# Queries on 128 partitions and token blocks by parity, in a fused attention and gated feed-forward kernel

## Chip, cores and metric

The kernel runs on one core of one Trainium2 chip. The metric is the device time of one execution in microseconds (us). It was 236.85 us before the change, the median of three runs (236.81 to 237.19). A profile of one execution gives the time of every instruction and of every DMA packet.

## What is computed

Eight batches, eight heads, 576 tokens, head size 64, 32 memory slots. Keys and values are first condensed to 32 memories per head by a softmax over `phi`; the queries attend to the memories; the heads are put side by side to 512 columns, and a gated feed-forward block of width 1536 follows.

```python
a    = softmax(phi, axis=2)                    # [b, h, s, 32]
k_m  = einsum('bhsm,bhsd->bhmd', a, k)         # [b, h, 32, 64]
v_m  = einsum('bhsm,bhsd->bhmd', a, v)
attn = softmax(q @ k_m^T / sqrt(64))           # [b, h, s, 32]
x    = (attn @ v_m) as [b * s, h * 64]         # [4608, 512]
out  = (silu(x @ w_gate) * (x @ w_val)) @ w_out
```

Inputs and output are float32 in memory; the loads of q, k, v and the weights cast to bfloat16 on the way.

## The kernel before

**Staging.** The program is written out by hand in its order (`manual_schedule`); each engine runs its own instructions in that order and waits on semaphores. The batches are pipelined. The prologue (lines 870 to 975) loads and prepares batches 0 and 1, with filler matmuls (`warm`) between; then both go through the first feed-forward half together. The main loop runs over b = 2 to 7. In each turn it makes the scores of batch b, in between runs matmuls of the last feed-forward product of batch b - 1, and then the 24 gate/value slots of batch b, into which the k/v sums and other preparations of batch b + 1 are spread.

**Queries.** A batch's q is loaded to `t_q` with a head's tokens on 96 partitions, six consecutive rows each (`P, J = 96, 6`). For batches 0 to 2 `load_q_group` loads it in two DMAs, even and odd heads, and later batches have one (`load_q`); all are on POOL's queue, in program order with phi, k, v and the weights. The scores need q with the head size on the partitions. For batches 0 to 2 TensorE transposes it (`q_T`, L381): four steps of six transposes of 96 x 128, each step for two pairs of heads into one PSUM bank, and a copy to `t_qT` by VectorE or ScalarE (L394, L392). From batch 3 on, one DMA transpose on SP's queue does it (`load_qT`, L121). A pair of rows (r = 0, 1) fills 128 partitions, so the columns of `t_qT` are tokens by row pair.

**Attention.** `scores(b, g)` (L404) makes eight matmuls for the even or the odd heads; ScalarE takes the exp (`t_E`, L415). The sum over the memories is inverted either by TensorE and ScalarE (`z_inv`, batches 0 and 1, `t_lz`) or by VectorE (`z_inv_v`), and `norm` multiplies (`t_A`, L455). `r` splits the tokens into two halves of 288.

**Feed-forward.** The condensed values are multiplied into the weights first (`u_round`, `u_item`, `u_three`: `p_u`, L475, emptied to `t_U` by L495 to L501). A slot (`gv_slot`, L518) makes a gate product, its silu on ScalarE (`t_sg`, L535), a value product, and VectorE's multiplication to `t_h` (L541). The last product goes by a scheme with seven instead of eight block products (`products`, L739): it needs sums and differences of blocks of `t_h` (`t_S`, L563, L605) and of `w_out` (`t_T`). A batch's 576 tokens make two blocks of 256; the remaining 64 of four batches together make a "quad" (`xs`, L595, `quad_sums`), done in batch 4's and in the last slots and at the end. Units of these products are taken from a list, `backlog`, and spread between the other work as filler. For batch 2 the list is set from the last product of batch 1:

```python
        if b == 2:
            norm(2, 1)
            u_three(2)
            backlog = one[36:]
```

**PSUM.** There are eight banks, handed out in the order in which they were given back (`bank`, `done`). Evacuated results go to `t_o` tiles with three buffers.

**Stores.** `store` (L699) splits 128 tokens at the borders of 96, so that a block of 128 leaves in two DMAs (96 and 32, 64 and 64, or 32 and 96 rows). They go out on SP's queue; in the last quad some of the stores of 64 tokens are on ScalarE's queue. In the last batch and the last quad, halves of 256 columns are stored on their own.

Of the kernel before, what the change touches and what calls it, by code (L numbers as in the profile page):

```python
# [14 lines left out]
def kernel(  # L15
# [23 lines left out]
    B, H, S, D = q.shape  # L39
    M = phi.shape[3]  # L40
    DM, DF = moe_w_gate.shape
    P, J = 96, 6
    JK = 9
    NG = 2
    NP = H // 2
# [15 lines left out]

    ctx.enter_context(tc.manual_schedule())

    out_r = out.rearrange("(b p j) c -> b j p c", b=B, p=P, j=J)


    phis, kvs, qs, qTs = {}, {}, {}, {}
# [33 lines left out]
    def load_v(b):  # L101
        nc.gpsimd.dma_start(out=kvs[b][:, 1], in_=head_pairs(v[b]))  # L102

    def load_q_group(b, g):

        if g == 0:
            qs[b] = inp.tile([P, NG, NP, J * D], BF16, tag=f"q{Q_SLOT[b]}", bufs=1, name="t_q")
        nc.gpsimd.dma_start(  # L108
            out=qs[b][:, g],
            in_=q[b].rearrange("(i g) (p j) d -> g p i (j d)", g=NG, p=P)[g],  # L110
        )

    def load_q(b):
        t = inp.tile([P, H, J * D], BF16, tag=f"q{Q_SLOT[b]}", bufs=1, name="t_q")
        nc.gpsimd.dma_start(out=t, in_=q[b].rearrange("h (p j) d -> p h (j d)", p=P))
        qs[b] = t

    def load_qT(b):

        t = att.tile([128, H, 3, P], BF16, tag="qT", name="t_qT")  # L120
        nc.sync.dma_start_transpose(  # L121
            out=t.rearrange("p h j t -> p (h j) t"),
            in_=qs[b].rearrange("p h f -> p (h f)"),
        )
        for i in range(NP):
            qTs[b, i] = t[:, 2 * i:2 * i + 2].rearrange("p h j t -> p h (j t)")

    W = {}

# [242 lines left out]
        done(p)  # L372
        scaled.add(b)

    def q_T(b, g, n, eng="v"):


        pq = bank([128, 2, HALF], BF16, "p_q")
        for i in range(2):
            for jj in range(3):  # L380
                nc.tensor.transpose(  # L381
                    pq[:, i, P * jj:P * (jj + 1)],
                    qs[b][:, g, 2 * n + i, 2 * D * jj:2 * D * (jj + 1)],
                    ident[0:P, 0:P],
                )
        if g == 0 and n == 0:
            box["qT"] = att.tile([128, H, 3, P], BF16, tag="qT", name="t_qT")
            for i in range(NP):
                qTs[b, i] = box["qT"][:, 2 * i:2 * i + 2].rearrange("p h j t -> p h (j t)")
        t = box["qT"].rearrange("p (i g) j t -> p g i (j t)", g=NG)[:, g, 2 * n:2 * n + 2]  # L390
        if eng == "a":
            nc.scalar.copy(out=t, in_=pq)  # L392
        else:
            nc.vector.tensor_copy(out=t, in_=pq)  # L394
        done(pq)

    def gv_banks():
# [2 lines left out]
    def scores(b, g):  # L400
        p = gv_banks()
        for i in range(NP):
            for r in range(2):
                nc.tensor.matmul(  # L404
                    p[r][32 * i:32 * i + 32, 0:HALF],
                    lhsT=kTs[b][64 * r:64 * r + 64, g, 32 * i:32 * i + 32],
                    rhs=qTs[b, i][64 * r:64 * r + 64, g],
                    start=True,
                    stop=True,
                    tile_position=(64 * r, 32 * i),  # L410
                )
        e = att.tile([128, 2, HALF], BF16, tag=f"E{g}", name="t_E")
        for r in range(2):
            scale = rks[b][:, g:g + 1] if b in rks else sm_scale
            nc.scalar.activation(out=e[:, r], in_=p[r][:, 0:HALF], func=AF.Exp, scale=scale)  # L415
        done(*p)
        es[b, g] = e
# [166 lines left out]
    def blocks(b, c):  # L584

        x = hts[b, c].rearrange("p (m e) t -> p e m t", e=2)
        return [x[:, e, :, 256 * n:256 * n + 256] for n in range(2) for e in range(2)]

    def chunk_done(b, c):

        if b % 2 == 0 and c == 0:
            xs[b // 2] = hpool.tile([128, NJF, 2, 64], BF16, tag="xs", name="t_x")

        def ends():
            nc.gpsimd.tensor_copy(  # L595
                out=xs[b // 2][:, 4 * c:4 * c + 4, b % 2], in_=hts[b, c][:, :, S - 64:S]
            )
# [12 lines left out]

        end = c + 1 == NCH
        fourth = b in (3, 7)
        if (b, c) in ((0, 2), (1, 1), (1, 2)):
            late.append(lambda *part: sums(nc.gpsimd if b else nc.vector, *part))
        elif b < 2:
            sums(nc.gpsimd)
        elif end:
            sums(nc.vector)
            if b + 1 == B:
                second.pop()(nc.vector, (2, 3))  # L620
                wait_for(Ss[b, 1][0:1, 3, 0, 0:1])
            else:
                wait_for(t[0:1, 3, 0, 0:1])
                second.pop()(nc.gpsimd, (3, 2))
        else:
            if c:
                sums(nc.gpsimd, (0, 1))
                second.append(sums)
            else:
                sums(nc.gpsimd)  # L630
        if end and b > 1 and not fourth:
            late.append(ends)
        else:
# [15 lines left out]
    def quad_sums(qd):  # L649
# [22 lines left out]
                    subtract(nc.gpsimd, t[:, 2], A12, t[:, 1])  # L672

    beside_sums = {
        (0, 0): lambda: (load_phi(3, nc.gpsimd), load_q_group(2, 0)),
        (1, 0): lambda: (load_q_group(2, 1), load_q(3)),
        (0, 1): lambda: (load_k(3), load_v(3)),
    }

    turn = [1]  # L680

    def token_segments(b, t0, count):
        segs = []
        t = t0
        while t < t0 + count:
            blk, pp = divmod(t, P)
            n = min(P - pp, t0 + count - t)
            segs.append((t - t0, n, b, 2 * (blk % 3) + blk // 3, pp))
            t += n
        return segs  # L690

    def store(t_o, b, t0, count, row=0, cols=slice(0, 512), queues=None):

        for r0, m, bb, jj, pp in token_segments(b, t0, count):
            eng = nc.sync
            if queues:
                turn[0] += 1
                eng = queues[turn[0] % len(queues)]
            eng.dma_start(out=out_r[bb, jj, pp:pp + m, cols], in_=t_o[row + r0:row + r0 + m])  # L699

    def products(b, by_hand, quad=None):

# [6 lines left out]
        def A(e, n):  # L709
            if quad is not None:  # L710
                return lambda c, m, u: xs[2 * quad + n][:, 4 * c + 2 * m + e].rearrange(
                    "p a t -> p (a t)"
                )
            return lambda c, m, u: hts[b, c][
                :, 2 * m + e, 256 * n + 128 * u:256 * n + 128 * u + 128
            ]

        def Sx(n):
# [52 lines left out]
                done(mine[home])  # L771

        def both(name, t0, cols):
            for u in range(U):
                store(mine[name][:, u, cols], b, t0 + 128 * u, 128, cols=cols)

        def c11():
            t = tile_of("o1", (128, 2, DM), tag="to")
# [17 lines left out]
            both("o2", 256, slice(0, DM))  # L796

        def leftover(name, room, half, cols):
            queues = dict(c22=(nc.scalar,), c21=(nc.scalar, nc.sync)).get(name) if end else None

            def run():
                if room:
# [12 lines left out]
                    done(home)  # L815
                for k in range(2):
                    x = 4 * quad + 2 * (name > "c20") + k
                    store(t, x, S - 64, 64, 64 * k, cols, queues)

            return run  # L820

# [18 lines left out]
        return first + five + six + three + seven + four, ops  # L840

    def q_items(b, evac):
        return [
            lambda g=g, n=n: q_T(b, g, n, evac[2 * g + n]) for g in range(NG) for n in range(2)
        ]

    def u_item(b, c, evac="avav"):

# [51 lines left out]
    load_phi(1, nc.scalar)  # L900
    exp_tables()
    load_k(0)
    for g in range(NG):
        load_q_group(0, g)
    load_k(1)
    nc.vector.memset(bones, 0.0)
    nc.vector.memset(ones1, 1.0)
# [6 lines left out]
    for b in range(2):  # L914
        phi_zeros(b, nc.vector)
        phi_exp_masked(b)
    for g in range(NG):
        load_q_group(1, g)
    load_v(0)
    load_v(1)  # L920
    for half in range(2):
# [14 lines left out]

    warm(104)
    k0, k1 = k_items(0, "vvvv"), k_items(1, "vvvv")
    q0, q1 = q_items(0, "vvvv"), q_items(1, "vvvv")
    run(k0)  # L940
    warm(8)
    run(k1[:1])
    warm(4)
    run(q0[:2])
    warm(2)
    scores(0, 0)
    run(q0[2:])
    warm(2)
    z_inv(0, 0)
    scores(0, 1)  # L950
# [1 line left out]
    run(k1[1:])  # L952
    warm(3)
    z_inv(0, 1)
    run(q1[:2])
    warm(2)
    scores(1, 0)
    norm(0, 0)
    run(q1[2:])
    norm(0, 1)  # L960
    warm(3)
    z_inv(1, 0)
# [175 lines left out]
```

## Time and profile before

| | |
|---|---|
| median of three runs | 236.85 us (236.81 to 237.19) |
| profiled execution, its own time | 236.93 us |
| its span in the profile | 235.1 us |
| TensorE matmuls | 225.3 us, 96% of the span, 2842 instructions |
| VectorE / ScalarE / POOL | 185.2 / 173.0 / 143.9 us (79 / 74 / 61%) |
| granted TensorE clock | 0.999 |
| DMA | 36.84 MB, 157 GB/s on average |
| loads of q | 5 DMAs of 576 KB, 6 of 288 KB |
| stores on SP's queue | 23 of 192 KB, 40 of 64 KB, 14 of 128 KB, two each of 96 and 32 KB |

Busy times overlap, since the engines work at the same time. The matmuls are pipelined and the end of each is modelled, so that 96% does not mean that TensorE is at its peak. What counts is the chain of work that ended last. The time outside the span, 1.8 us, lies before and after the profiled instructions.

### The profile page before, as it was taken

To read this page: it belongs to the slowest core of one execution; us is meant where nothing else is said; L and a number is where in the kernel's file an instruction comes from. 1 tells how busy PE (TensorE), PEld (TensorE's weight loads), DVE (VectorE), ACT (ScalarE), POOL (GpSimd) and SP (SyncE) were. 2 spreads that over 40 slices of the span, in tenths; PEclk is the share of its full clock that TensorE was granted. 3 is DMA by queue.
4 is the path that set the end of the run, shared out by engine and by line. 5 is a ranking of instruction groups with operands and counts; after the bars stand their busy time and mean duration, and the time that the engine had idled before them with its cause. 6 is when DMAs were issued, how large, how long until landed. Compare 5 with 4: busy or idle time off the path is not lost.

```text
span 235.1 us, 7317 instructions
## 1 busy us (share of the span) xinstructions
PE 225.3 (96%) x2842; PEld 170.5 (73%) x2842; DVE 185.2 (79%) x425; ACT 173.0 (74%) x368; POOL 143.9 (61%) x193
## 2 busy tenths in 40 slices
PE   7998899999999999999999999999999999999992
PEld 2555467778886677887788787887788778878881
DVE  4157699999976797999798667998799879977732
ACT  2758889987447888978896668978898789677220
POOL 8542526999099069664976689464845494039390
PEclk9999999999999999999999999999999999999999
DMA  6999999999996992999199945999022803212125
GB/s 208 205 205 207 198 208 207 225 239 249 206 195 168 251 222 22 268 219 189 31 191 249 237 132 85 246 230 121 6 86 74 142 0 93 60 46 76 42 62 167
DMA packets 42594, 36.84 MB, mean 157 GB/s; under 512 B 15424, under 2 KB 37952, under 8 KB 42560
## 3 DMA queue, kind: packets, MB, share of 16 engines
q0 software_dynamic: 21440, 22.42, 54.4%
q1 hardware_dynamic: 20352, 13.18, 25.0%
q10 hardware_dynamic: 768, 0.79, 1.0%
q8 instruction: 22, 0.36, 0.6%
q14 instruction: 12, 0.10, 0.1%
HBM read 42.47 MB, written 9.44 MB: 221 GB/s over the span
## 4 chain that ended last, share of the span: by engine, by line
PE 86%; DMA 8%; POOL 2%; DVE 1%; issue 1%; POOLq 0%
PE p_g L518 21%; PE p_v L518 21%; PE p_os L739 20%; PE p_oc L739 10%; DMA t_kv<-in_v_dram 8%; PE p_u L475 5%; PE p_oa L739 5%; PE p_kv L234 2%; POOL t_q L108 1%; PE p_g L404 1%; POOL t_kv L98 1%; PE p_q L381 0%; DVE t_bkv L270 0%; POOL t_kv L102 0%; PE p_mT L323 0%
## 5 line engine op out<-in xcount | busy, mean ns | idle before, releaser
L541 DVE TENSOR_TENSOR t_h<-t_sg,p_v 128x288 bf16<-128x288 bf16 x192 | 82.2, 452 | 17.6 <-PE p_v L518 7.2
L518 PEld LDWEIGHTS <-t_U 128*128 128x128 bf16 x768 | 73.7, 98 | 23.9 <-issue 3.3
L535 ACT ACTIVATE t_sg<-p_g 128x288 bf16<-128x288 f32 x192 | 74.3, 423 | 18.4 <-PE p_g L518 12.0
L518 PE MATMUL p_g<-t_A,t_U 128*128 128x288 bf16 x384 | 77.4, 286 | 1.1 <-DVE t_U L499 0.7
L518 PE MATMUL p_v<-t_A,t_U 128*128 128x288 bf16 x384 | 77.2, 286 | 0.0
L739 PEld LDWEIGHTS <-t_S 128*128 128x128 bf16 x384 | 37.4, 98 | 4.5 <-issue 0.2
L605 POOL TENSOR_TENSOR t_S<-t_h 128x512 bf16<-128x512 bf16 x17 | 19.6, 1154 | 31.4 <-DVE t_h L541 31.4
L739 PEld LDWEIGHTS <-t_h 128*128 128x128 bf16 x288 | 26.9, 98 | 8.9 <-issue 5.3
L495 ACT CAST t_U<-p_u 128x512 bf16<-128x512 f32 x53 | 28.0, 607 | 6.9 <-PE p_u L475 6.9
L739 PE MATMUL p_os<-t_T,t_S 128*128 128x256 bf16 x192 | 23.7, 273 | 0.0
L563 POOL TENSOR_TENSOR t_S<-t_S,t_h 128x512 bf16<-128x512 bf16 x17 | 19.6, 1154 | 1.3
L563 POOL TENSOR_TENSOR t_S<-t_h 128x512 bf16<-128x512 bf16 x16 | 18.4, 1150 | 0.0
L563 POOL TENSOR_TENSOR t_S<-t_h,t_S 128x512 bf16<-128x512 bf16 x16 | 18.4, 1150 | 0.0
L475 PE MATMUL p_u<-W,t_kT 64*32 64x512 bf16 (+1 forms) x416 | 15.9, 363 | 0.1
L739 PE MATMUL p_os<-t_T,t_h 128*128 128x256 bf16 x96 | 15.3, 274 | 0.0
L889 PE MATMUL p_warm<-bones 128*128 128x512 bf16 (+2 forms) x43 | 12.8, 427 | 1.7 <-DVE bones L912 1.7
L499 DVE CAST t_U<-p_u 128x512 bf16<-128x512 f32 x19 | 12.4, 684 | 2.0 <-PE p_u L475 2.0
L739 PE MATMUL p_oc<-t_T,t_S 128*128 128x256 bf16 x96 | 12.0, 273 | 0.0
L739 PE MATMUL p_oa<-WO,t_h 128*128 128x256 bf16 x96 | 11.8, 273 | 0.0
L739 PE MATMUL p_oc<-WO,t_S 128*128 128x256 bf16 x96 | 11.8, 272 | 0.0
L739 PE MATMUL p_os<-WO,t_h 128*128 128x256 bf16 x96 | 11.8, 272 | 0.0
L455 DVE TENSOR_TENSOR t_A<-t_E,t_lz 128x576 bf16<-128x576 bf16 x16 | 11.4, 740 | 0.3 <-ACT t_lz L431 0.3
(107 smaller groups left out, 315.1 us busy)
## 6 DMA issues: line engine op xcount, KB each, us to landing
t_kv<-in_k_dram POOLq DMA_DIRECT2D x8, 576.0 KB, 11.0
t_kv<-in_v_dram POOLq DMA_DIRECT2D x8, 576.0 KB, 14.9
out_dram<-t_o SPq DMA_DIRECT2D x23, 192.0 KB, 2.6
t_phi<-in_phi_dram POOLq DMA_DIRECT2D x6, 576.0 KB, 9.9
t_q<-in_q_dram POOLq DMA_DIRECT2D x5, 576.0 KB, 8.5
out_dram<-t_o SPq DMA_DIRECT2D x31, 64.0 KB, 2.3
out_dram<-t_o SPq DMA_DIRECT2D x14, 128.0 KB, 3.7
t_q<-in_q_dram POOLq DMA_DIRECT2D x6, 288.0 KB, 11.4
```

The source lines that it names most:

```text
L234: nc.tensor.matmul(p[g][32 * i:32 * i + 32, 0:n], lhsT=phi_of(b, g, j, i), rhs=kvs[b][64 * g:64 * g + 64, w0:w1, i, j * D:(j + 1) * D], st ...
L455: nc.vector.tensor_tensor(out=a, in0=es.pop((b, g)), in1=lzs.pop((b, g)), op=ALU.mult)
L475: nc.tensor.matmul(p[g][32 * i:32 * i + 32, o:o + n], lhsT=kTs[b][64 * g:64 * g + 64, 2, 32 * i:32 * i + 32], rhs=w_part(w, c, i, g, halve ...
L495: nc.scalar.copy(out=t, in_=p)
L499: nc.vector.tensor_copy(out=t, in_=p)
L518: nc.tensor.matmul(p[:, 0:HALF], lhsT=Us[b, c, g][:, o // 2, which, 128 * (o % 2):128 * (o % 2 + 1)], rhs=atts[b, g][:, r], start=(g == 0) ...
L535: nc.scalar.activation(out=sg, in_=gate[:, 0:HALF], func=AF.Silu)
L541: nc.vector.tensor_tensor(out=dst, in0=sg, in1=val[:, 0:HALF], op=ALU.mult)
L563: eng.tensor_tensor(out=out, in0=x, in1=y, op=ALU.subtract)
L605: eng.tensor_tensor(out=t[:, 0], in0=A21, in1=A22, op=ALU.add)
L739: nc.tensor.matmul(mine[home][:, u], lhsT=lhs(c, m, u), rhs=rhs(c, m), start=fresh and u == 0, stop=(k == 5), skip_group_check=u == 1 or n ...
L889: nc.tensor.matmul(p[:, 0:128 * a], lhsT=bones, rhs=x.to_broadcast([128, a, 128]) if a > 1 else bones, start=True, stop=True,)
```

## The change

A partition of `t_q` now holds 36 consecutive rows of a head: partition 16 h + c has the rows 36 c to 36 c + 35 of head h, so that a batch's q is one contiguous [128, 2304] array and comes in one DMA. Two consecutive rows (r = 0, 1) are 128 columns; 18 such column blocks (s) are transposed as 128 x 128 squares, in three steps of six for batches 0 to 2 and by one DMA transpose for the others. The scores of a head read 16 columns from each of the 18 blocks (`q_of`). Token 36 c + 2 s + r now stands at r * 288 + 16 s + c. The two blocks of 256 tokens are thus those with even and with odd rows (r), s below 16; the remainder is s = 16 and 17 of both. A block of 128 tokens (eight s, sixteen c) is stored by one DMA, and so are the remainder's 64 tokens of one batch; in the last quad the first batch's go on SP's and the second's on ScalarE's queue. Last, the six remaining units of batch 1's last product are run before batch 2's slots instead of being spread into them.

```diff
-    out_r = out.rearrange("(b p j) c -> b j p c", b=B, p=P, j=J)
+    out_r = out.rearrange("(b c s r) k -> b r s c k", b=B, c=NC, s=NS)      # NS, NC = 18, 16
...
+    def load_q(b):
+        t = inp.tile([128, NS * 128], BF16, tag=f"q{Q_SLOT[b]}", bufs=1, name="t_q")
         nc.gpsimd.dma_start(
+            out=t,
+            in_=q[b].rearrange("h s d -> (h s d)").rearrange("(p f) -> p f", p=128),
         )
...
     def load_qT(b):
+        qTs[b] = att.tile([128, NS, 128], BF16, tag="qT", name="t_qT")
+        nc.sync.dma_start_transpose(out=qTs[b], in_=qs[b])
+
+    def q_of(b, i, g, r):
+        h = NG * i + g
+        return qTs[b][64 * r:64 * r + 64, :, NC * h:NC * h + NC]
...
+    def q_T(b, n, eng="v"):
+        k = NS // 3
+        pq = bank([128, k, 128], BF16, "p_q")
+        for x in range(k):
+            y = k * n + x
+            nc.tensor.transpose(pq[:, x], qs[b][:, 128 * y:128 * y + 128], ident)
+        if n == 0:
+            qTs[b] = att.tile([128, NS, 128], BF16, tag="qT", name="t_qT")
+        copy(eng, qTs[b][:, k * n:k * n + k], pq)
         done(pq)
...
-                    rhs=qTs[b, i][64 * r:64 * r + 64, g],
+                    rhs=q_of(b, i, g, r),
...
-        return [x[:, e, :, 256 * n:256 * n + 256] for n in range(2) for e in range(2)]
+        return [x[:, e, :, HALF * n:HALF * n + 256] for n in range(2) for e in range(2)]
...
-                out=xs[b // 2][:, 4 * c:4 * c + 4, b % 2], in_=hts[b, c][:, :, S - 64:S]
+                out=xs[b // 2][:, 4 * c:4 * c + 4, b % 2].rearrange(
+                    "p o (s r t) -> p o s r t", s=2, r=2
+                ),
+                in_=hts[b, c].rearrange("p o (r s t) -> p o s r t", r=2, s=NS)[:, :, 16:],
...
+    def store_block(t_o, b, n, cols):
+        for u in range(2):
+            nc.sync.dma_start(out=out_r[b, n, 8 * u:8 * u + 8, :, cols], in_=t_o[:, u, cols])
+
+    def store_leftover(t_o, b, cols, eng):
+        rows = out_r[b, :, 16:NS, :, cols].rearrange("r s c k -> s r c k")
+        eng.dma_start(out=rows.rearrange("s r c k -> (s r) c k"), in_=t_o)
...
-            queues = dict(c22=(nc.scalar,), c21=(nc.scalar, nc.sync)).get(name) if end else None
+            engs = (nc.sync, nc.scalar) if end else (nc.sync, nc.sync)
...
-    q0, q1 = q_items(0, "vvvv"), q_items(1, "vvvv")
+    q0, q1 = q_items(0, "vvv"), q_items(1, "vvv")
...
-    run(q0[:2])
+    run(q0)
     warm(2)
     scores(0, 0)
-    run(q0[2:])
...
-    run(q1[:2])
+    run(q1)
     warm(2)
     scores(1, 0)
     norm(0, 0)
-    run(q1[2:])
...
-            kv, q2 = kv_items(2), q_items(2, "aava")
+            kv, q2 = kv_items(2), q_items(2, "aaa")
...
-            backlog = one[36:]
+            run(one[36:])
```

More of the change, by code (lines that the diff above doesn't have):

```diff
@@ L41 @@
     DM, DF = moe_w_gate.shape
-    P, J = 96, 6
+    NS, NC = 18, 16
     JK = 9
@@ L102, in load_v @@
         nc.gpsimd.dma_start(out=kvs[b][:, 1], in_=head_pairs(v[b]))
-    def load_q_group(b, g):
-        if g == 0:
-            qs[b] = inp.tile([P, NG, NP, J * D], BF16, tag=f"q{Q_SLOT[b]}", bufs=1, name="t_q")
+    def load_q(b):
+        t = inp.tile([128, NS * 128], BF16, tag=f"q{Q_SLOT[b]}", bufs=1, name="t_q")
         nc.gpsimd.dma_start(
-            out=qs[b][:, g],
-            in_=q[b].rearrange("(i g) (p j) d -> g p i (j d)", g=NG, p=P)[g],
-        )
-    def load_q(b):
-        t = inp.tile([P, H, J * D], BF16, tag=f"q{Q_SLOT[b]}", bufs=1, name="t_q")
-        nc.gpsimd.dma_start(out=t, in_=q[b].rearrange("h (p j) d -> p h (j d)", p=P))
+            out=t,
+            in_=q[b].rearrange("h s d -> (h s d)").rearrange("(p f) -> p f", p=128),
+        )
         qs[b] = t
     def load_qT(b):
[L120 to L126, printed above, removed]
+        qTs[b] = att.tile([128, NS, 128], BF16, tag="qT", name="t_qT")
[3 more added lines that the diff above has]
+        return qTs[b][64 * r:64 * r + 64, :, NC * h:NC * h + NC]
     W = {}
@@ L373, in v_direct @@
         scaled.add(b)
[L375 to L394, printed above, removed]
+    def q_T(b, n, eng="v"):
[7 more added lines that the diff above has]
+        copy(eng, qTs[b][:, k * n:k * n + k], pq)
         done(pq)
@@ L674 @@
     beside_sums = {
-        (0, 0): lambda: (load_phi(3, nc.gpsimd), load_q_group(2, 0)),
-        (1, 0): lambda: (load_q_group(2, 1), load_q(3)),
+        (0, 0): lambda: (load_phi(3, nc.gpsimd), load_q(2)),
+        (1, 0): lambda: load_q(3),
         (0, 1): lambda: (load_k(3), load_v(3)),
     }
[L680 to L699, printed above, removed]
+    def store_block(t_o, b, n, cols):
[4 more added lines that the diff above has]
+        eng.dma_start(out=rows.rearrange("s r c k -> (s r) c k"), in_=t_o)
     def products(b, by_hand, quad=None):
@@ L714, in A @@
             return lambda c, m, u: hts[b, c][
-                :, 2 * m + e, 256 * n + 128 * u:256 * n + 128 * u + 128
+                :, 2 * m + e, HALF * n + 128 * u:HALF * n + 128 * u + 128
             ]
@@ L773, in both @@
         def both(name, t0, cols):
-            for u in range(U):
-                store(mine[name][:, u, cols], b, t0 + 128 * u, 128, cols=cols)
+            store_block(mine[name], b, t0 // 256, cols)
         def c11():
@@ L817, in run @@
                     x = 4 * quad + 2 * (name > "c20") + k
-                    store(t, x, S - 64, 64, 64 * k, cols, queues)
+                    store_leftover(t[64 * k:64 * k + 64], x, cols, engs[k])
             return run
@@ L842, in q_items @@
     def q_items(b, evac):
-        return [
-            lambda g=g, n=n: q_T(b, g, n, evac[2 * g + n]) for g in range(NG) for n in range(2)
-        ]
+        return [lambda n=n: q_T(b, n, evac[n]) for n in range(3)]
     def u_item(b, c, evac="avav"):
@@ L902 @@
     load_k(0)
-    for g in range(NG):
-        load_q_group(0, g)
+    load_q(0)
     load_k(1)
@@ L916 @@
         phi_exp_masked(b)
-    for g in range(NG):
-        load_q_group(1, g)
+    load_q(1)
     load_v(0)
```

## Prediction

> **What bounds the kernel now.** I read the page first, then the chain in order of time, the timelines of the start and of the end, the windows by stage and the single DMA packets of the trace. The page's chain is TensorE almost throughout, and its only large other piece is the load of v at the start:
>
> ```profile
> PE 86%; DMA 8%; POOL 2%; DVE 1%; issue 1%; POOLq 0%
> 6.87 18.00 DMA t_kv<-in_v_dram
> ```
>
> So a change counts in three places only: what sets when the first gate products start (about 27 us), holes in TensorE's stream, and what follows the last matmul. From 26 us on TensorE waited for something visible in two places, together 1.0 us, both in one hole. The chain in order of time shows it where batch 2's slots begin, and the list of TensorE's waits names the longer part:
>
> ```profile
> 74.80 0.63 PE p_u L475 x16
> 75.66 0.48 issue
> 76.13 0.69 DVE t_U L499
> 76.88 0.54 PE p_g L518 x3
> PE p_g L518 <- DVE t_U L499: 0.7, 1, 0.7
> ```
>
> The start, from its timeline (start, duration, engine, operation): q's transposes, their copies, the first exps, and ScalarE's table load that ends its chain.
>
> ```profile
> 12.61 0.67 PE L381 MATMUL p_q<-ident,t_q 96*128 96x96 bf16 x12
> 13.06 0.82 DVE L394 COPY t_qT<-p_q 128x576 bf16<-128x576 bf16 x2 [0.36 <-PE p_q L381]
> 14.28 0.50 ACT L415 ACTIVATE t_E<-p_g,t_rk 128x288 bf16<-128x288 f32 x1 [3.39 <-PE p_v L404]
> 19.57 0.50 ACT L415 ACTIVATE t_E<-p_g,t_rk 128x288 bf16<-128x288 f32 x1 [0.41 <-PE p_v L404]
> 24.42 1.28 ACT L967 ACT_TABLE_LOAD   x1
> ```
>
> The end, from its timeline: after the last copy there are only stores, and SP issues them one by one, 0.59 us each.
>
> ```profile
> 229.77 1.19 ACTq L699 DMA_DIRECT2D out_dram<-t_p  x2
> 230.64 0.42 DVE L337 COPY t_q<-p_os 128x256 f32<-128x256 f32 x1 [0.30 <-PE p_os L739]
> 230.78 1.77 SPq L699 DMA_DIRECT2D out_dram<-t_q  x3
> 231.14 0.47 ACTq L699 DMA_DIRECT2D out_dram<-t_q  x1
> ```
>
> **Part 1: q in 18 square blocks, at the start.** TensorE's work is the same: 24 transposes of 96 columns at 0.042 us (12 in 0.67 us less 0.21 of latency) against 18 of 128 at 0.055, 1.0 us either way. What changes is the dependence. Before, the copy of two head pairs let half of the scores go. After, each score matmul reads 16 columns of all 18 blocks, so it needs all three copies. A copy of 576 columns takes 0.45 us and one of 384 (L293) 0.35, so one of 768 takes 0.54; two in a row overlap by 0.08. Batch 0: first block at 13.1, copies to 13.13 + 0.47 + 0.47 + 0.54 = 14.61, first exp at 15.1 instead of 14.28: 0.8 late. Batch 1: VectorE casts its k sums until 18.32, now 19.1; then the three copies, to 20.6; first exp 21.0 instead of 19.57: 1.43 late. From 19.57 ScalarE is nearly dense to the end of the table load at 25.70, so that ends at 27.1; it can empty the first p_u then instead of at 26.41, 0.7 late. VectorE's last norm ends at 26.6 and its casts of v at 27.6 instead of 26.69, 0.9 late. The first gate product needs both: I take 0.85 us. Ends: 0.6 (the earlier copies catch up in the gaps) and 1.4 (ScalarE's whole delay). After it TensorE runs without holes to 75 us, so nothing gives it back.
>
> The loads: q arrives in 128 packets instead of 768. The packets of 768 B take 79 ns and those of 1152 B 107, which makes one of 4608 B some 360 ns, eight per engine: up to 0.9 us less per load by sums of packets, some 0.3 by the distance between packets (61 and 88 ns). v and the weights land that much earlier, but this is worth nothing, because ScalarE and VectorE are late by more. It keeps W's later landings from becoming a new wait.
>
> **Part 2: `run(one[36:])` ahead of batch 2's slots.** Twelve matmuls of 0.109 us, 1.31 us, move from the slots into the hole, which is 1.35 us from the end of u_three's streaming (75.4) to 76.88 less one gate matmul of 0.12. There they are free. In the slots (76.9 to 93.2) TensorE is full while ScalarE has 13.7 and VectorE 13.0 of 16.3 us, so the time comes out, with one exception: four of the matmuls covered the wait after the k/v sums, where banks come free only when kv_norm ends (82.74). That cover, 0.4 us, is lost. ScalarE's copy for c21 goes ahead of the first silu (0.5 us), which the eight banks absorb. Gain 0.95 us, ends 1.3 and 0.4.
>
> **Part 3: the scores' strided reads.** The moving operand now comes in runs of 32 bytes. The nearest row, L323's rhs, has runs of 64 bytes and 36 matmuls in 0.65 us, no sign of a penalty. I take 0. At half speed each wave of 0.13 us doubles, six pairs: 0.8 us. The weights' and POOL's pieces (L595 with runs of 16) have slack: POOL is 61% busy.
>
> **Part 4: stores between.** SP's stores fall from 81 to 46, two instead of four for each pair of 128-token blocks; SP is on no path before the end. One risk: c22 of batch 1 writes the buffer that o1 of batch 0 stores from. That store would land about 75, the write is due at 75.7. I take 0, far end 0.5 us.
>
> **Part 5: the last stores.** Two opposite things. SP now issues five stores after 227.97 instead of seven; its last one goes at 231.1 instead of 232.0: 0.85 us earlier. ScalarE's queue gets the second half of the remainder's c11 ahead of the last silu: silu 1.1 late, VectorE's product 0.65, the mark on POOL 0.65, the last quarter sums 229.9 instead of 229.26, and TensorE's product that reads them waits 0.3 us. So the end moves by -0.55 us if the data of a store takes as long as today.
>
> But the store's shape changes. Every transfer in the trace has 32, 64, 96 or 128 outermost on both sides and leaves sixteen 4-byte completion packets (q0: 704 for 44 transfers; q10: 64 for 4): it is dealt to 16 engines. On the DRAM side the new stores have 8 outermost (s) over 16 (c), the remainder 4 over 16; no row shows such a one. Near end: dealt to 16 like today's 64 KB stores (2.1 us to landing). Far end: one engine per outermost entry. I take the far end, the nearest to the rows: what is dealt there is always equal shares of outermost entries, and 8 or 4 cannot be dealt to 16. If the first engines take them each time, the four busiest get, from the first packet of the last c12 (227.5): 32 packets of 1 KB (c12), 32 of 2 KB (c21) and six remainder stores of 16 each. A 1 KB packet takes 46 to 60 ns there, one of 2 KB 84 to 106. Low: 128 x 0.046 + 32 x 0.084 = 8.6 us; high: 128 x 0.060 + 32 x 0.106 = 11.1 us. The last packet ends at 236.1 to 238.6 instead of 233.66, so the end is 2.4 to 4.9 us later; with fewer engines there is less contention at the memory, so I take 3.0. The 0.3 us wait hides in this.
>
> [...]
>
> **Sum.** +0.85 - 0.95 + 0 + 0 + 3.0 = +2.9 us. The profiled execution took 236.93 us, 1.83 around its span of 235.1, and lies 0.08 above the median of 236.85. 236.93 + 2.9 = 239.8 us.
>
> **Rivals.**
> A, faster: the stores stay on 16 engines. Then +0.85 - 0.95 - 0.55 = -0.65, 236.3 us. For it: half of SP's issues go, and SP's backlog is what ends last now. Against it: the outermost 8 and 4. It decides if a remainder store still lands within about 2.3 us of its issue.
> B: the stores stay on 16, but the start costs its full 1.4, or the hole's filler its low end: -0.55 + 1.4 - 0.4, or with half-speed scores 0.8 more: 237.3 to 238.2 us. Against it: eight banks and a nearly unchanged TensorE order.
> C: the copies of q don't delay the start because v's landing (24.9) still rules. Then forecast and A are 0.85 lower. Against it: v's casts on VectorE stand behind the norms that come late.
>
> **How the numbers follow.** Forecast 0.72 (its own range 238.2 to 241.9: the tail's 2.4 to 4.9 and 0.85's and 0.95's ends); A 0.15; B 0.10; C alone, in A's or the forecast's place, 0.03. No change means within 0.2%, 0.47 us, about what a measurement here can tell. Faster: two thirds of A and some of C and of a tail below its low end: 0.14. Same: the rest of A, a little of B: 0.07. Slower 0.79. The range leaves out A's lower half and the far tails: 236.5 to 241.9.
>
> **What would show it.** Right: exps of batch 1 near 21.0; the first gate product near 27.9; no hole before batch 2's slots; the last remainder stores landing 4 us or more after issue while TensorE ends within 1 us of 230.6; the 64 KB remainder stores with fewer than 16 completion packets. Wrong: landings near 2.3 us (then A), TensorE's end beyond 232 (then parts 1 to 4 are off).

## The result and the profile after

The changed kernel takes 244.48 us (median of six runs, 242.87 to 245.83) against 236.83 us before (six runs, 236.74 to 237.19): a ratio of 1.032, 95% interval 1.028 to 1.036. Its runs spread over 3.0 us, those of before over 0.45. The profiled execution is the fastest of the six: 242.87 us, span 240.9.

In the names below, c11, c12, c21 and c22 are the four blocks of a last product's result, and the remainder (the 64 tokens of each batch outside the blocks of 256) has four of its own. "L503" is a line of the changed kernel.

The lines that answer to those of before. First the page's chain, then three lines of the list of TensorE's waits (total, times, longest):

```profile
PE 87%; POOL 3%; DVE 3%; ACT 2%; issue 1%; POOLq 0%
```

```profile
PE p_g L389 <- DVE t_qT L332: 1.6, 2, 0.8
PE p_oc L716 <- issue: 0.9, 1, 0.9
PE p_oc L716 <- POOL t_Q L548: 0.7, 3, 0.2
```

v's load has left the chain. Three waits of TensorE are new: the first scores for VectorE's copies, 0.9 us in the middle of the program for "issue" (nothing that the profile shows), and the last products for POOL's quarter sums (`t_Q`). The hole before batch 2's slots is gone, as the chain in order of time shows; the twelve moved matmuls stand in it:

```profile
75.24 0.77 PE p_u L460 x24
76.04 1.47 PE p_os L716 x12
77.52 0.49 PE p_g L503 x4
```

The start, from its timeline:

```profile
12.70 1.49 DVE L332 COPY t_qT<-p_q 128x768 bf16<-128x768 bf16 x3 [0.45 <-PE p_q L376]
14.25 0.29 PE L389 MATMUL p_g<-t_qT,t_kT 64*32 64x288 bf16 x1 [0.80 <-DVE t_qT L332]
20.61 0.50 ACT L400 ACTIVATE t_E<-p_g,t_rk 128x288 bf16<-128x288 f32 x1 [1.18 <-PE p_v L389]
25.30 1.28 ACT L937 ACT_TABLE_LOAD   x1
27.36 1.32 PE L503 MATMUL p_g<-t_A,t_U 128*128 128x288 bf16 x8
```

The stall in the middle, from TensorE's timeline:

```profile
136.85 0.49 PE L716 MATMUL p_oc<-t_T,t_Q 128*128 128x256 bf16 x3
138.28 0.39 PE L716 MATMUL p_oc<-t_T,t_Q 128*128 128x256 bf16 x2 [0.93 <-issue]
```

And the end, from its timeline:

```profile
218.56 1.40 ACTq L676 DMA_DIRECT2D out_dram<-t_o  x1
220.06 0.41 ACT L520 ACTIVATE t_sg<-p_g 128x288 bf16<-128x288 f32 x1 [2.22 <-DMA out_dram<-t_o]
223.35 0.18 POOL L635 COPY t_mark<-t_S 1x1 bf16<-1x1 bf16 x1 [5.94 <-DVE t_S L548]
231.86 0.42 DVE L785 TENSOR_TENSOR t_q<-p_oc,t_q 128x256 f32<-128x256 f32 x1 [1.39 <-PE p_oc L716]
232.52 0.42 DVE L332 COPY t_q<-p_os 128x256 f32<-128x256 f32 x1 [0.23 <-PE p_os L716]
232.32 1.80 ACTq L676 DMA_DIRECT2D out_dram<-t_q  x2
```

One store on ScalarE's queue holds up the last silu, POOL's mark stands at 223.35 instead of 221.24, VectorE's t_q waits 1.39 us for products that wait for POOL, and the last copy starts 1.88 us later than before (230.64). Its data then takes until 239.41, 6.9 us after the copy's start; before it took 3.0 (233.66).

Shift of TensorE's stream against before, place by place: +0.39 us at the first gate product, -0.59 from 90 us on (the hole), +0.52 after the stall, +0.41 from 183, +0.62 at 222, +1.88 at the last copy, +5.75 at the last packet.

### The profile page after: what moved, and what is told of

It reads as the page before. It is cut to its first block, busy times and chain, and to the rows that moved or that the text cites. A ratio compares the mean times of both kernels' runs of the same rounds, so it can differ in the third digit from the quotient of the medians.

```text
span 240.9 us, 7224 instructions
## 1 busy us (share of the span) xinstructions
PE 225.5 (94%) x2824; PEld 169.9 (71%) x2824; DVE 183.8 (76%) x422; ACT 173.3 (72%) x368; POOL 140.1 (58%) x190
## 4 chain that ended last, share of the span: by engine, by line
PE 87%; POOL 3%; DVE 3%; ACT 2%; issue 1%; POOLq 0%
PE p_g L503 20%; PE p_v L503 20%; PE p_os L716 18%; PE p_oc L716 8%; PE p_oa L716 5%; PE p_u L460 5%; PE p_warm L863 4%; PE p_kv L229 2%; POOL t_Q L548 2%; DVE t_qT L332 1%; ACT t_E L400 1%; PE p_g L389 1%; PE p_mT L318 1%; PE p_q L376 1%; POOL t_Q L654 1%
## 5 line engine op out<-in xcount | busy, mean ns | idle before, releaser
L503 PEld LDWEIGHTS <-t_U 128*128 128x128 bf16 x768 | 73.6, 98 | 23.2 <-issue 4.0
L503 PE MATMUL p_g<-t_A,t_U 128*128 128x288 bf16 x384 | 77.2, 286 | 0.2
L503 PE MATMUL p_v<-t_A,t_U 128*128 128x288 bf16 x384 | 77.2, 286 | 0.0
L716 PEld LDWEIGHTS <-t_h 128*128 128x128 bf16 x288 | 27.1, 98 | 8.6 <-issue 5.0
L716 PE MATMUL p_os<-t_T,t_h 128*128 128x256 bf16 x96 | 14.8, 273 | 0.0
## 6 DMA issues: line engine op xcount, KB each, us to landing
t_kv<-in_k_dram POOLq DMA_DIRECT2D x8, 576.0 KB, 11.1
```

The costliest lines, as they stand in the source:

```text
L503: nc.tensor.matmul(p[:, 0:HALF], lhsT=Us[b, c, g][:, o // 2, which, 128 * (o % 2):128 * (o % 2 + 1)], rhs=atts[b, g][:, r], start=(g == 0) ...
L716: nc.tensor.matmul(mine[home][:, u], lhsT=lhs(c, m, u), rhs=rhs(c, m), start=fresh and u == 0, stop=(k == 5), skip_group_check=u == 1 or n ...
```

## The experiments

"Time" is the median, with the lowest and highest run, "ratio" that to the kernel before on the same chip, with its 95% interval. Theory F: the end is late because the new stores are carried by 8 and 4 DMA engines. Rival R: because they are fewer and issued later.

**1. All stores on 16 engines.** A block now takes every second c instead of eight neighbouring s, so that 16 s are outermost in memory; the remainder is kept in the order c, s, r.

```diff
-                :, 2 * m + e, HALF * n + 128 * u:HALF * n + 128 * u + 128
+                :, 2 * m + e, HALF * n + u:HALF * n + 256:2
-            nc.sync.dma_start(out=out_r[b, n, 8 * u:8 * u + 8, :, cols], in_=t_o[:, u, cols])
+            nc.sync.dma_start(out=out_r[b, n, 0:16, u::2, cols], in_=t_o[:, u, cols])
-                    "p o (s r t) -> p o s r t", s=2, r=2
+                    "p o (t s r) -> p o s r t", s=2, r=2
-        rows = out_r[b, :, 16:NS, :, cols].rearrange("r s c k -> s r c k")
+        rows = out_r[b, :, 16:NS, :, cols].rearrange("r s c k -> c s r k")
```

> The changed kernel with every store spread over the 16 DMA engines again: a block takes every second class c of the 16 (stationary operand read with step 2), so that the 16 pairs s are outermost in the 128-token store; the remainder rows are kept in the order c, s, r, so that the 16 classes are outermost there. Same number of stores, same bytes, same queues. Theory F (the stores' few engines make the tail): the last copy still ends near 232.9, the last packet comes about 3 us after the last copy's start as in the kernel before (230.64 to 233.66), so near 235.6 instead of 239.4; the span is near 237.0 and the time near 239.0, 238.4 if the 1.1 us stall at 137 us goes too; the runs lie within 0.6 us of each other. Rival R (the stores are late because they are fewer and issued later, not because of the engines): the last packet stays within 1 us of 239.4 and the time at 242 to 244.

237.72 us (236.98 to 238.94), ratio 1.003 (1.001 to 1.005). F holds, and more than expected: the last copy starts at 232.13, nearly as late as in the changed kernel, and the last packet ends at 234.48, 2.35 us after it. The stall at 137 us is gone as well. But the runs still spread over 2 us, in two groups (five at 236.98 to 237.47, five from 237.97 on), which theory F doesn't explain. The granted clock divides them the same way: 0.995 to 0.998 over the whole run in the five faster ones, 0.989 to 0.991 in the five slower. The profiled run is one of the slower, and its windows show where (columns: length; busy time with instruction count of TensorE matmuls, weight loads, VectorE, ScalarE, POOL; granted clock; DMA):

```profile
19.33:22.74 3.41, 2.15 (x27) 0.79 (x25) 2.43 (x5) 2.13 (x6) 0.79 (x2) 1.00 1.22 205
22.74:26.16 3.42, 3.36 (x43) 1.84 (x42) 1.96 (x6) 3.02 (x7) 1.23 (x2) 0.50 1.45 199
```

For 3.41 us the clock was granted at half, right after a window with the 0.80 us wait for q's copies in it. The first gate product comes at 28.41.

**2 and 3. Only the blocks, or only the remainder, on 16 engines** (each one half of that diff).

> Only the 128-token stores on 16 engines, the remainder stores still on 4. Theory F: the last eight 2 KB-row stores land by 233 instead of 235.06, but the last two remainder stores still put 96 packets of about 50 ns on each of 4 engines from about 234.2 on, so the last packet stays near 239 and the time near 242.3. If the stall at 137 us (TensorE waits for nothing shown) is a code load held up by block stores on 8 engines, it is gone here: then 241.5 and a smaller spread of runs. Rival R: as F in the end, but the stall stays.

> Only the remainder stores on 16 engines, the 128-token stores still on 8. Theory F: the last 2 KB stores still end near 235.1 on 8 engines; the last remainder stores have 24 packets per engine (1.1 us), on those 8 engines behind them: last packet near 236.3, time near 239.8, stall at 137 us as in the changed kernel. Rival R: last packet within 1 us of 239.4, time 242 to 244.

Blocks alone: 240.30 us (239.51 to 240.73), ratio 1.013 (1.011 to 1.016), 1.2 us below F's 241.5; no stall; last packet at 237.27 instead of F's 239, 4.6 us after the last copy's start (232.63) instead of run 1's 2.35: what is left of the tail goes with the remainder's stores on four. Remainder alone: 243.96 us (243.18 to 246.16), ratio 1.031 (1.026 to 1.036), a miss for F's 239.8 and inside rival R's 242 to 244, but not for R's reason. In its trace the tail is shorter (4.7 us from copy to last packet instead of 6.9), but the stall has grown, by TensorE's timeline:

```profile
139.15 0.49 PE L716 MATMUL p_oc<-t_T,t_Q 128*128 128x256 bf16 x3
142.65 0.39 PE L716 MATMUL p_oc<-t_T,t_Q 128*128 128x256 bf16 x2 [3.00 <-issue]
```

and the window after it is again at half clock (143.97 to 147.39). So the stall goes with the block stores, and its length varies from trace to trace.

**4. c11's remainder store back on SP.**

```diff
-            engs = (nc.sync, nc.scalar) if end else (nc.sync, nc.sync)
+            engs = (nc.sync, nc.scalar if end and name != "c11" else nc.sync)
```

> Changed kernel with one store moved: the remainder store of c11 of the last batch is issued by SP instead of from ScalarE's queue, so that it no longer stands 1.40 us ahead of the last silu. Theory: the last silu starts near 217.9 instead of 220.06, POOL's quarter sums end near 229.5 instead of 231.4, TensorE waits for none of them, the last copy starts near 231.3 instead of 232.5 and the last packet comes 1.2 us earlier, near 238.2: time near 241.7 in its best run. Rival (the stores' engines are busy to the end anyway): the last copy is earlier but the last packet moves by less than 0.4 us, since the 2 KB stores fill the engines to 235 us first.

243.74 us (242.35 to 244.45), ratio 1.026 (1.023 to 1.029). The mechanism is there: TensorE no longer waits for t_Q, and this line of VectorE's timeline had 1.39 us of idle time in the changed kernel:

```profile
232.84 0.42 DVE L785 TENSOR_TENSOR t_q<-p_oc,t_q 128x256 f32<-128x256 f32 x1 [0.19 <-PE p_oc L716]
```

From TensorE's shift of 2.92 us at 228 us to the last copy nothing is added (233.55 against 230.64 + 2.92). The last packet ends at 241.09. Counted from TensorE's shift ahead of the end (2.92 here, 0.41 in the changed kernel), the last copy comes 1.48 us earlier and the last packet 0.83, between the theory's 1.2 and the rival's 0.4: 0.65 us of the gain is lost between the copy and the last packet, and that the busy engines hold it up there is inferred. Its worth in the time drowns in the spread here; run 9 against run 8 gives it.

**5 and 6. The holes at the start filled; and, on top, the blocks of all batches but the last on 16 engines.**

```diff
     run(q0)          # and the same behind run(q1)
-    warm(2)
+    warm(14)
```

> The changed kernel with one edit: twelve more units (three 512-column matmuls, 0.65 us) of warm-up work behind the q transposes of batches 0 and 1, in the two 0.80 us holes in which TensorE waits for VectorE's three copies. Theory C (the holes let the clock gate close for one window of 3.41 us in most runs, which costs 1 to 1.7 us on top of the wait): the clock stays at 1.00 from 6 to 230 us of the start stage in the profiled run, the first gate product is again 0.4 us later than before's and not 1.4 to 2.6, the lowest time stays near 242.9 and the median comes down from 244.5 to about 243.3. Rival N (the drop is noise of the chip, or the spread comes from the stores alone): median stays within 0.4 us of 244.5 and the first gate product at 28.4 or later in the profiled run.

> As the run with filled holes, and the 128-token stores of all batches but the last on 16 engines; those of the last batch stay on 8 and the remainders on 4. Theory L (TensorE's stall at 137 us is its own next chunk of 16 KB of instructions, queued on an engine that the stores fill): the stall of 1.1 to 3.3 us is gone and the instruction packet there starts before 135 us of the before kernel's clock; TensorE stands 0.6 us ahead of before's at 180 us instead of 0.5 behind; the tail is as in the changed kernel, so the time is 1.1 to 1.5 us below the run with filled holes, near 241.8. Rival (the stall is something else of that place, such as the wait for a bank): it stays, and the time is within 0.4 us of the run with filled holes.

Run 5: 244.95 us (244.27 to 247.72), ratio 1.036 (1.032 to 1.041). The clock stays open through the start, but it opened late, at 7.0 us, and the first gate product is 1.14 us behind before's instead of 0.4; and the median is no lower: this trace has a stall of 2.73 us and half clock from 140.1 to 143.5. The expectation was wrong in taking the start for the main part of the spread. Run 6: 242.40 us (241.75 to 242.48), ratio 1.022 (1.021 to 1.024): 2.6 us less, no stall, and the spread is down to 0.7 us. So the block stores of the batches between cause the stall, as theory L says; TensorE is level with before at 180 us, not 0.6 us ahead as expected, since this start is 0.94 us late. What the single packets show of the way from one to the other (us):

| trace | q's DMA transpose, last packet | 16 KB instruction packet | ends | TensorE goes on | stall |
|---|---|---|---|---|---|
| before | 135.26 | 131.92 | 132.88 | | none |
| changed | 136.02 | 135.81 | 137.03 | 138.28 | 0.93 |
| 3 | 140.22 | 139.99 | 141.21 | 142.65 | 3.00 |
| 4 | 138.20 | 137.96 | 139.19 | 140.44 | 0.94 |
| 5 | 138.07 | 137.84 | 139.07 | 140.30 | 2.73 |
| 1 (16 engines) | 137.43 | 134.08 | 135.47 | | none |
| 2 (16 engines) | 137.03 | 134.93 | 136.10 | | none |
| 6 (16 engines) | 136.41 | 134.31 | 135.48 | | none |
| 9 (16 engines) | 136.75 | 133.01 | 134.47 | | none |

In the four stalls the packet starts 0.2 us before the end of q's transpose, and TensorE goes on 1.2 to 1.4 us after the packet's end. All four traces stop after the same count of TensorE's instructions from the start, the 1,756th matmul. Run 5 has six warm-up matmuls more ahead, and it stops six matmuls earlier in the program, between the two of a gate product instead of between two of `p_oc`:

```profile
137.28 0.29 PE L503 MATMUL p_g<-t_A,t_U 128*128 128x288 bf16 x1
140.30 0.42 PE L503 MATMUL p_g<-t_A,t_U 128*128 128x288 bf16 x1 [2.73 <-issue]
```

So the stall hangs on the count of instructions, as it would if the next piece of the program had not arrived, and not on what the program waits for at that place; a wait for a bank or a buffer would have stayed with its place in the program.

The timeline of SP's queue has the transpose behind the block stores. In the changed kernel:

```profile
125.57 1.26 SPq L671 DMA_DIRECT2D out_dram<-t_o  x2
126.94 7.49 SPq L116 DMA_TRANSPOSE t_qT<-t_q  x1
```

The transpose's own length doesn't separate the runs. It takes 5.56 us before, 7.49 here and 8.79 in run 5, but also 7.88 in run 9, on 16 engines and without a stall; and in run 1 it ends at 137.43, later than here. What differs is where the packet stands: 2.1 to 3.7 us ahead of the transpose's end in the 16-engine rows of the table, 0.2 in the stalled ones. What the packet itself waited for is not shown, since no record here names the engine that carried it. The page lists the packet's queue as "q8 instruction", with 22 packets and 0.36 MB both before and in the changed kernel. That it is TensorE's is inferred: TensorE runs 5,648 of the 7,224 recorded instructions of the changed kernel.

**7. The kernel before, with `run(one[36:])` alone.**

```diff
-            backlog = one[36:]
+            run(one[36:])
```

> The kernel before with one edit of the change: the last third of batch 1's output products is run ahead of batch 2's slots instead of being kept as a backlog. Theory: the 1.3 us hole before the slots is filled and four or five covers are lost later, -0.95 in the sum of the prediction, -1.0 in the changed kernel's trace: 236.05 against 237.05. Rival (the covers that are missing later let TensorE wait as long elsewhere): within 0.3 us of before.

236.04 us (235.81 to 236.33) against 236.91, ratio 0.996 (0.995 to 0.998): -0.87. In the trace TensorE is 0.97 us ahead from 100 us on. By its median this is the fastest version of all.

**8 and 9. The changed kernel with all three repairs, and without c11's.** 8 is runs 1, 4 and 5 together, 9 is runs 1 and 5.

> The changed kernel with all three repairs: all stores on 16 engines, c11's remainder store on SP, the holes at the start filled. Start +0.4, hole before batch 2's slots -1.0, no stall, quarter sums of POOL 0.36 us longer by the strided writes of the remainder copies: TensorE ends near 230.2 instead of 230.60, the last packet comes 2.4 us after the last copy's start (as in the run with all stores on 16 engines), near 232.8, so the span is near 234.3 and the time near 236.2, faster than before by 0.8 us. Rival (quarter sums still late, or the strided stationary reads cost something): 236.7 to 237.3.

> All stores on 16 engines and the two 0.80 us holes at the start filled with warm-up work; c11's remainder store still on ScalarE's queue. Theory C (the holes close the clock gate in half of the runs): no window at half clock after the start in the profiled run, all runs within 0.8 us of each other, median near 237.0, the undisturbed half of the runs with 16 engines (236.98 to 237.47), instead of 237.72; TensorE still waits twice or three times for t_Q near 230 us. Rival N: the spread of 2 us and the median of 237.7 stay. Against the run with all repairs (236.36) it shows what c11's store on ScalarE's queue costs: 0.6 to 0.7 by theory, under 0.2 if the late quarter sums were hidden.

Run 8: 236.36 us (236.06 to 237.17), ratio 0.998 (0.997 to 0.999), so faster than before by 0.2%, and 0.3 us slower than run 7. Its tail is better than that of before: last copy at 230.10, last packet at 232.46, 2.36 us instead of 3.02. Run 9: 237.67 us (237.05 to 238.06), ratio 1.003 (1.002 to 1.004). No window at half clock, spread halved from 1.96 to 1.01 us, but the median is not that of run 1's faster group (237.12), as expected, but 0.55 above it. Against run 8 c11's store costs 1.3 us by the medians, twice what was expected. In the two traces it is 0.94: ahead of the last products TensorE is 0.30 us behind run 8, a difference of the start, and at the last copy 1.24 (231.34 against 230.10). VectorE's timeline has the wait again:

```profile
230.69 0.42 DVE L785 TENSOR_TENSOR t_q<-p_oc,t_q 128x256 f32<-128x256 f32 x1 [1.19 <-PE p_oc L716]
```

Against run 6, which differs in the last batch's and the remainder's stores alone (and in the order in which POOL's copies write the remainder), 16 engines are worth 4.7 us.

**10 to 12. Two tries to win back the start.** 10: batch 0's second q copy on ScalarE. 11: the same, with four instead of twelve units of fill behind batch 0's transposes. 12: besides, 16 units less of the first warm-up.

```diff
-    q0, q1 = q_items(0, "vvv"), q_items(1, "vvv")
+    q0, q1 = q_items(0, "vav"), q_items(1, "vvv")
-    warm(104)
+    warm(88)         # run 12 only
```

> The kernel with all three repairs, and the second of batch 0's three q copies on ScalarE (0.80 us there, idle from 10.6 to 14.6 us) instead of VectorE (0.55 us). Theory (the three copies in a row on VectorE are what makes the first scores late): the first score matmuls come 0.35 us earlier, the exps of both batches and the first gate product follow by 0.2 to 0.35 us: 236.05 against 236.36. Rival (v's landing or the order on VectorE rules the first gate product): the first gate product moves by less than 0.1 us, time 236.3 to 236.5.

> As the run with batch 0's second copy on ScalarE, but with four units of warm-up work behind batch 0's transposes instead of twelve: there the fill had taken the place of the wait (the first scores waited 0.15 us for the warm-up matmuls). Theory: the first scores now come 1.70 to 1.75 us after the first q transpose instead of 2.07, the first gate product 0.3 us earlier after the first p_S product than in the run with all repairs (17.6 instead of 18.0 us). Time 236.05, or 235.9 if the clock opens early. Rival: the exps of batch 1 wait for something else, so the distance from p_S to the first gate product stays at 17.9 or more and the time at 236.4.

> The same with 16 units (four matmuls, 0.87 us at full clock) less of warm-up work at the very start. Theory P (in the changed start the whole chain hangs on when the warm-up ends, since v's landing no longer ends it): the first p_S product and all after it come 0.5 to 0.9 us earlier, until v's landing ends the chain again (first gate product near 26.9 as in the kernel before): time 235.6 to 235.8. Rival (k's or q's landing ends it then): within 0.15 us of the run with the whole warm-up.

10: 236.64 us (236.16 to 237.16), ratio 0.999 (0.998 to 0.999); by TensorE's timeline my fill had taken the place of the wait, so it says nothing on the copies:

```profile
14.97 0.28 PE L389 MATMUL p_g<-t_qT,t_kT 64*32 64x288 bf16 x1 [0.15 <-PE p_warm L863]
```

11: 236.38 us (235.93 to 237.05), ratio 0.998 (0.996 to 0.999), the same as run 8. The first scores do come 0.25 us earlier after the first transpose (1.82 instead of 2.07 us; 1.70 to 1.75 was expected), but the first gate product stands 18.02 us behind the first p_S product, as in run 8 (18.11): the rival's side, since batch 1's transposes wait 0.25 us for q's load. 12: 236.44 us (235.64 to 238.71), ratio 0.998 (0.996 to 1.000). The rival was right: the first p_S product came at 8.40 instead of the changed kernel's 9.32, at nearly the same opening of the clock (5.2 and 5.3 us), but then TensorE waited for q's load, and the clock was at half from 12.0 to 15.4 (a row of the timeline and one of the windows):

```profile
11.87 2.00 PE L376 MATMUL p_q<-ident,t_q 128*128 128x128 bf16 x18 [0.60 <-DMA t_q<-in_q_dram]
11.99:15.41 3.42, 3.27 (x29) 2.09 (x27) 1.12 (x2) 1.04 (x2) 1.23 (x2) 0.50 1.19 219
```

## Why the prediction was wrong

Slower was right, and so was the reason with the largest price; the time was 4.7 us too low, beyond the range. Two steps failed: part 4 put the stores between at nothing (2.6 us measured), and part 5 took the end too low, c11's store by 0.9 to 1.3 us and the few engines by about 1. By its own steps:

| step | forecast | measured, with the place |
|---|---|---|
| 1, start | +0.85 (0.6 to 1.4) | +0.39 in the profiled run; +0.83 counted from p_S |
| 2, hole | -0.95 | -0.98 in the trace, -0.87 alone (run 7) |
| 3, strided score reads | 0 | 0 (a score matmul takes 289 ns, before 289) |
| 4, stores between | 0 (to 0.5) | 2.6 (run 5 against 6), with run 5's half clock from 140.1 to 143.5 |
| 5, c11 on ScalarE's queue | 0.3, hidden | 0.94 in the traces, 1.3 by medians (run 9 against 8) |
| 5, fewer stores, had they 16 engines | -0.85 | -0.66 from copy to last packet (run 8) |
| 5, few engines, against the end of before | +2.4 to +4.9, 3.0 taken | +3.9 from copy to last packet; 4.7 less the 0.66 above by runs 6 and 9, so 4.1 |

**Part 4 failed.** "SP is on no path before the end" looked only at who waits for a store. It left out what else the stores can hold up. The runs show 2.6 us in its place: with block stores on eight engines TensorE stands still for 0.9 to 3.0 us at a fixed count of its instructions, right behind a late 16 KB packet, and with 16 engines it doesn't. That the packet holds its next instructions is inferred, though the fixed count (the 1,756th matmul) leaves little else; what delays the packet stays open. The far end of 0.5 us priced a buffer, which was not the cost.

**Part 5 was mis-sized twice.** The chain of c11's store was named link by link, but silu was 2.4 us late instead of 1.1 (220.06 against 217.62) and the mark 2.1 instead of 0.65; 0.4 of each had come from further ahead. The store could only be issued at 218.56, when VectorE had written c11 (218.11 to 218.53), 0.5 us after the silu was due; the issue itself took 1.40 us, and the slack that the prediction took off was not there. And "the 0.3 us wait hides in this" let the wait and the stores overlap, where they add: the last remainder data cannot leave before the last product. The engines' own price lay inside the stated range, but at 3.9 to 4.1 and not at 3.0. The last six remainder stores alone, 384 packets of 1 KB, so 96 on each of four engines, ran from 234.42 to 239.41, 52 ns each, inside the 46 to 60 of the sum. The eight-engine c21 stores, 256 packets of 2 KB, so 32 on each, ran from 230.59 to 235.06, 140 ns each instead of 84 to 106. No run shows the lighter contention at the memory for which 3.0 was taken: the median 2 KB packet of the last stores took 84 ns before and after. That fewer engines carry the stores has two measurements behind it. SP's queue q1 has 624 completion packets of 4 bytes, and 1040 with the same DMAs in run 1; the difference, 416, is what 34 block stores with 8 and 12 remainder stores with 4 lack to 16 each (34 x 8 + 12 x 12). And the windows give a DMA share of 0.43 from 230.60 to 235.06 us and of 0.24 from there to 239.41, the time of 6.9 and 3.8 of 16 engines; before, it was 0.78 from 231.00 to 233.66, the time of 12.5. That the first engines take every store, on which the sum of 8.6 to 11.1 us rests, no run shows, since no record names an engine; the 0.24, with stores on two queues at once, fits four engines in all, and from c12's first packet at 228.54 to the last at 239.41 the stores took 10.87 us.

**Part 1 was right in mechanism, and incomplete.** The exps of batch 1 came at 20.61 (forecast near 21.0), the table load ended at 26.58 (forecast 27.1); both stand 0.44 us later, at 21.05 and 27.02, when they are counted from the first p_S product, which itself came 0.44 us earlier than before. The first gate product follows the first p_S product by 18.04 us, before by 17.21, which is the 0.83. But p_S (the sums of the softmax over `phi`) itself moves with the moment the clock opens, which differs between executions:

| trace | clock opens | first p_S | first gate | distance | half clock in the start |
|---|---|---|---|---|---|
| before | 6.2 | 9.76 | 26.97 | 17.21 | none |
| changed | 5.3 | 9.32 | 27.36 | 18.04 | none |
| 1 | 5.7 | 9.51 | 28.41 | 18.90 | 22.7 to 26.2 |
| 2 | 6.2 | 9.78 | 28.56 | 18.78 | 23.3 to 26.7 |
| 3 | 7.4 | 10.38 | 29.48 | 19.10 | 17.7 to 21.1 |
| 4 | 7.7 | 10.49 | 29.52 | 19.03 | 17.9 to 21.3 |
| 5, filled | 7.0 | 10.14 | 28.11 | 17.97 | none |
| 6, filled | 6.5 | 9.94 | 27.91 | 17.98 | none |

Before, TensorE waited 0.80 us for v's landing, which can take up a late p_S; the change removed that wait by making everything else later, so a late opening now goes through to the first gate product: in the rows of the changed start without half clock the distance is 17.97 to 18.04, for a p_S from 9.32 to 10.14. That this slack is why the runs of before spread by only 0.4 to 0.6 us is argued, not shown. On top of it, the two waits of 0.80 us cost another 0.7 to 1.1 us in the rows where the clock drops to half. Rival C, with v's landing in charge, is excluded: TensorE no longer waits for it.

**The sum.** In the profiled run: +0.39 - 0.98 + 1.11 (stall) - 0.11 + 0.21 + 1.26 (quarter sums) + 3.87 (stores) = +5.75. The median lies 1.6 us above that run; longer stalls and windows at half clock, as in runs 3 to 5, are of that size, but the other five runs have no trace. The separate runs give about as much as the medians' 7.65: +0.83 - 0.87 + 2.6 + 0.94 to 1.3 + 4.1 = 7.6 to 8.0. They leave out the half clock at the start and were taken in different versions, so part of this agreement is luck. Rivals A and B are excluded: completion packets, and run 1. The prediction's sign "TensorE's end beyond 232" came (the last copy starts at 232.52), and it pointed at parts 1 to 4; 1.26 us of that delay were part 5's c11, and 1.11 part 4's stall.

## What to carry to other kernels

Before changing the order of rows, look at what stands outermost on the memory side of each store: 8 or 4 there cost some 7 us in this kernel (2.6 and 4.7), and a block of every second class instead of neighbouring ones restored 16 (1040 completion packets on q1 instead of 624) at no cost in the weight loads (97.8 ns, 97.7 without). A DMA that nobody waits for can still cost time: here stores in mid-kernel made TensorE stand still for 0.9 to 3.0 us with no releaser in the profile. A stall at the same count of instructions in versions whose programs differ ahead of it (here the 1,756th matmul in four traces) speaks against a wait of that place in the program; that it was the fetch of instructions is inferred. Before a new wait in the warm-up is called short, see what the clock does behind it: in runs 1 to 4 it was at half for 3.41 us behind waits of 0.8 to 0.9 us, and in runs 5 and 6, with these waits filled, it was not.

## What the runs showed of the hardware

- **TensorE stood still without a releaser at a fixed count of its instructions.** It stood for 0.9 to 3.0 us with "issue" as its releaser, until 1.2 to 1.4 us after a 16 KB packet of the queue "q8 instruction", each time after its 1,756th matmul. That the packet holds its instructions is inferred.
- **The clock dropped to half behind partly busy windows.** A drop lasted 3.41 us (22.74 to 26.16 in run 1, 143.97 to 147.39 in run 3). In runs 1 to 4 the 3.41 us before the half clock at the start had 2.04 to 2.16 us of matmuls, with waits of 0.8 to 0.9 and 0.35 to 0.4 us; before the half clock in mid-kernel it was 1.32 (run 3) and 0.89 (run 5), and in run 12 it was 2.70. In the changed kernel's profile two such windows, with 2.09 (12.13 to 15.54) and 2.15 (18.96 to 22.37) and waits of 0.80 and 0.35 to 0.40 us, were followed by no drop, so neither the amount nor the waits alone tell when it comes.
- **A stationary operand read with step 2 cost nothing measurable**: weight loads took 97.8 ns in run 1, 97.7 without. POOL's copy of the remainder, written with step 4 (run 1), took 0.75 us instead of 0.40 (medians).
